# Causal attention and a hard-swish block on one core: five token groups become four of 448

## The chip, the cores and the metric

The kernel runs on one core of one Trainium2 chip. The metric is the device time of one execution in microseconds (us), as the median of several executions. TensorE (PE) multiplies; VectorE (DVE), ScalarE (ACT) and GpSimd (POOL) do elementwise work; SyncE (SP) issues every DMA of this kernel.

## The reference

Causal attention over 4 batches, 12 heads, 448 tokens and 64 dimensions a head, all in fp32, and behind it two matrix products with a hard-swish between them over the 1792 tokens:

```
scores = (q @ k.T) / 8, with -1e9 above the diagonal
attn   = exp(scores - rowmax) / (rowsum + 1e-9)
x      = (attn @ v), the heads side by side: 1792 x 768
h      = x @ w_in                      # 768 x 2048
g      = h * clip(h + 3, 0, 6) / 6
out    = g @ w_out                     # 2048 x 768
```

## The kernel before

**Tokens.** A sequence is cut into four blocks of C = 112 tokens, S = 448, R = 336. The two products behind the attention (the FFN from here on) are done for groups of tokens, with the weights stationary and the tokens of the group as the columns that stream. Group 0 holds the first block of all four batches (448 columns). Groups 1 to 4 hold blocks 1 to 3 of one batch each (336 columns).

**Attention.** Heads are taken two at a time (NPAIR = 6 pairs). `first_pair(p)` (L297) does group 0's attention for one pair, where only the diagonal blocks count. `pair(n)` (L410) does blocks 3, 2 and 1 of one batch and one pair: the scores (`products`, L445: matmuls L450 and L451, or L453), a masked row maximum on DVE (L476), the exponential on ACT (L483), the reciprocal of the row sums on DVE (L492, L493), the scaling on POOL (L505), the transposes of the 112x112 blocks on PE (L516), their eviction to SBUF (`move`, L238 or L241), and attention times V (`times_v`, L535). For batch 0 the scores are plain fp32 matmuls of 64 rows a head (L453). For batches 1 to 3 the operands are split into a rounded and a rest part (tiles op and kl, lines L245 and L250) and two matmuls a head and block do the product. The 64-row and 64-column matmuls (L453, L535, L399) use PE as several smaller arrays; the planner charges `SWITCH` for going to or from that mode (`tiled`). `x_split` (L277) evicts the result and splits it into xh and xl.

**FFN.** `group(g)` (L602) makes the group's two products. Every product of 128x128 weights with the tokens is three matmuls, high with high (L598), high with rest (L599), rest with high (L600). The up projection takes 16 chunks of weights with 18 matmuls each, the down projection 6 outputs with 48 each: 576 matmuls a group. `weights` (L547) loads a chunk of weights and splits it into wh (ACT) and wl (POOL or DVE). In group 0 DVE also decodes the words in which the weights arrive (L571, L573, L576), and the decoded ones are stored (kept_w) and loaded again by the later groups.

**Order.** Nothing runs in program order. Every piece of work is an `Op` with a key, the engines that may do it, a planned duration and its buffers. `Flow.run` plays the kernel through as a list schedule: a free engine takes the ready operation of the lowest key whose buffers (`BUFS`, L54; PSUM banks, `BANKS`, L58) are free, and the order that comes out is emitted for each engine. The keys count FFN steps: a group has 96 steps of six matmuls, group g begins at key 96 g. `pair(n)` begins at `T_EARLY + 13 * n` for batch 0 and at `T_REST + 16 * n` after it, its attention times V stands 15.9 steps later, its loads 24 steps before (`T_LOAD`). `first_pair(p)` begins at `T_FIRST + 8 * p`. So the attention of group g fills in between the FFN steps of group g-1.

```
T_FIRST, T_EARLY, T_REST, T_LOAD, T_W, T_WLOAD = -66, 4, -16, -24, 9, 9
t = T_FIRST + 8 * p
t = T_REST + 16 * n if b else T_EARLY + 13 * n
```

Of the kernel before, what the change touches and what calls it, by code (L numbers as in the profile page):

```python
# [33 lines left out]
F32R = mybir.dt.float32r  # L34
# [16 lines left out]
T_FIRST, T_EARLY, T_REST, T_LOAD, T_W, T_WLOAD = -66, 4, -16, -24, 9, 9  # L51
# [3 lines left out]
    gh=1, gl=1, prow=3, r=4, qk=4, op=3, kl=3, vr=3, wh=3, wl=3, pr3=4, pr2=3, pr1=3,  # L55
    pt0=4, pt1=4, pt2=4, wd=4, xh=8, xl=8,
# [134 lines left out]
def tile_causal_attention_hardswish_moe(ctx: ExitStack, tc: tile.TileContext, q, k, v, w_in, w_out, out):  # L191
# [85 lines left out]
    def x_split(key, g, p, av, n):  # L277
        xh, xl = buf("xh", [128, S], F32R), buf("xl", [128, S], F32R)
        x_t[g, p] = xh, xl
        move(key, n, lambda: ap(xh)[:, :n], lambda: ap(av)[:, :n], [(av, 0)], [(xh, 0)], {"A": 1, "D": (1, .5)})  # L280
        y = av
        if g < 2:
            y = buf("r", [128, S])
            move(key, n, lambda: ap(y)[:, :n], lambda: ap(av)[:, :n], [(av, 0)], [(y, 0)], {"A": 1})
        minus(
            key + .01, n, lambda: ap(xl)[:, :n], lambda: ap(y)[:, :n], lambda: f(ap(xh)[:, :n]),
            [(y, 0), (xh, 0)], [(xl, 0)], {"P": 2.4, "D": (1, 1.0)} if g < 2 else {"D": 1},
        )
# [8 lines left out]
    def first_pair(p):  # L297
        t = T_FIRST + 8 * p
# [11 lines left out]
        pr, ph = [buf("pr3", [C, S]) for _ in range(2)], [buf("pt0", [C, S]) for _ in range(2)]  # L310
# [97 lines left out]
    TILES = (3, 2, 1)  # L408

    def pair(n):  # L410
        b, p = divmod(n, NPAIR)
        t = T_REST + 16 * n if b else T_EARLY + 13 * n
        vr = buf("vr", [C, NC_, 2, D])
        qk = [buf("qk", [128, R + S]) for _ in range(2 if b else 1)]
        for e, x in enumerate(qk):
            for src, c0, c1 in ((q, C, 0), (k, 0, R)):
                n = S - c0
                for u in range(2):
                    dma(
                        t + T_LOAD, 256 * n, lambda x=x, u=u, c1=c1, n=n: ap(x)[64 * u:64 * u + 64, c1:c1 + n],  # L420
                        lambda e=e if b else u, src=src, c0=c0: src[b, p, e, :, c0:], w=[(x, u, c1)],
                    )
        dma(t + T_LOAD, 230e3, lambda: ap(vr), lambda: v[b, p], w=[(vr, 0)])
        raw = [(x, u, c1) for x in qk for u in range(2) for c1 in (0, R)]
        op, kl = [[buf(a, [128, w], F32R) for _ in qk] for a, w in (("op", R + S), ("kl", S))]
        if b:
            for e in range(2):
                x, y, z = qk[e], op[e], kl[e]
                move(
                    t - 5, R + S, lambda x=x, y=y: ap(y), lambda x=x: ap(x), raw[4 * e:4 * e + 4] + [("step", t - 12)], [(y, 0), (y, 1)],  # L430
                    {"P": 1.3, "A": (1, .5)},
                )
                minus(
                    t - 4.9, S, lambda z=z: ap(z), lambda x=x: ap(x)[:, R:], lambda y=y: f(ap(y)[:, R:]),
                    [(x, 0, R), (x, 1, R), (y, 1)], [(z, 0)], {"D": 1.25, "P": (2.2, 1.5)},
                )
                minus(
                    t - 4.8, R, lambda y=y: ap(y)[64:, :R], lambda x=x: ap(x)[64:, :R], lambda y=y: f(ap(y)[64:, :R]),
                    [(x, 1, 0)], [(y, 0)], {"D": 1.3, "P": (2.6, 1.5)},
                )  # L440
        st = buf("prow", [C, 2, 8])
        ps = {(e, i): bank("s") for i in TILES for e in range(2)}
        pr = {(e, i): buf(f"pr{i}", [C, C * (i + 1)]) for i in TILES for e in range(2)}

        def products(i, heads=(0, 1)):  # L445
            w, c = C * (i + 1), slice(C * (i - 1), C * i)
            for e in heads:
                dst, m = ap(ps[e, i])[:C, :w], slice(64 * e, 64 * e + 64)
                if b:
                    nc.tensor.matmul(dst, ap(op[e])[:, c], ap(op[e])[:, R:R + w], start=True, stop=False)  # L450
                    nc.tensor.matmul(dst, ap(op[e])[:, c], ap(kl[e])[:, :w], start=False, stop=True)  # L451
                else:
                    nc.tensor.matmul(dst, ap(qk[0])[m, c], ap(qk[0])[m, R:R + w], start=True, stop=True)  # L453

        for j, tiles in enumerate(((3, 2), (1,))):
            if b:
                for i in tiles:
                    for e in range(2):
                        pe(
                            t + 2 * j + .01 * e, [(.907e-3 * C * (i + 1), lambda i=i, e=e: products(i, (e,)), [(ps[e, i], 0), ("turn",)])],  # L460
                            [(op[e], 0), (op[e], 1), (kl[e], 0)],
                        )
            else:
                pe(
                    t + 2 * j,
                    [((1.68 * C * (i + 1) + 170) / 1000, lambda i=i: products(i), [(ps[0, i], 0), (ps[1, i], 0), ("turn",)])
                     for i in tiles],
                    raw, True,
                )
            for i in tiles:  # L470
                w = C * (i + 1)
                for e in range(2):
                    dst = lambda e=e, i=i, w=w: ap(ps[e, i])[:C, :w]
                    one(
                        t + 2 * j + .1, {"D": 1}, elem(w) + .2,
                        lambda _, e=e, i=i, w=w, dst=dst: nc.vector.tensor_tensor_reduce(  # L476
# [5 lines left out]
                        t + 2 * j + .2, {"A": 1}, (w + 300) / 1200 + .25,  # L482
                        lambda _, e=e, i=i, dst=dst: nc.scalar.activation(  # L483
# [6 lines left out]
        def inverse(_):  # L490
            r = ap(st)[:, :, 5:8]
            nc.vector.tensor_scalar_add(r, r, 1e-9)  # L492
            nc.vector.reciprocal(r, r)  # L493

        sums = [(st, e, 4 + i) for e in range(2) for i in TILES]
        one(t + 4, {"D": 1}, .45, inverse, [], sums)
        pt = {}
        for e in range(2):
            for i in reversed(TILES):
                def scaled(g, e=e, i=i):  # L500
                    x, r = ap(pr[e, i]), ap(st)[:, e, 4 + i:5 + i]
                    if g == "A":
                        nc.scalar.mul(x, x, r)
                    else:
                        nc.gpsimd.tensor_scalar(x, x, r, 1.0, ALU.mult, ALU.mult)  # L505
                one(
                    t + 4.5 + .1 * e, {"P": 1}, min(.95, .2 + C * (i + 1) / 500), scaled,
                    [(st, e, 4 + i)], [(pr[e, i], 0)],
                )
            for a, js in enumerate(((0,), (1,), (2, 3))):  # L510
                blocks = [(i, j) for j in js for i in range(max(j, 1), NC_)]
                tp, ph = bank("s"), buf(f"pt{js[0]}", [C, S] if js[0] == 0 else [C, R])

                def turn(e=e, blocks=blocks, tp=tp):
                    for o, (i, j) in enumerate(blocks):
                        nc.tensor.transpose(ap(tp)[:C, C * o:C * o + C], ap(pr[e, i])[:, C * j:C * j + C], ident)  # L516

                key = t + 6 + 3 * e + a
                pe(key, [(.3, turn, [(tp, 0)])], [(pr[e, i], 0) for i in {i for i, _ in blocks}])
                move(  # L520
                    key + .1, R, lambda ph=ph: ap(ph)[:, :R], lambda tp=tp: ap(tp)[:C, :R],
                    [(tp, 0)], [(ph, 0)], {"A": 1, "D": (1, .4)} if b else {"A": 1},
                )
                o = 0
                for j in js:
                    w = R if j == 0 else S - C * j
                    pt[e, j] = ph, o, w
                    o += w
        av = bank("s")

        def times_v():
            for j in range(NC_):
                for e in range(2):
                    ph, o, w = pt[e, j]
                    nc.tensor.matmul(  # L535
                        ap(av)[64 * e:64 * e + 64, R - w:R], ap(vr)[:, j, e, :], ap(ph)[:, o:o + w],
                        start=(j == 0), stop=(j == NC_ - 1),
                    )
# [63 lines left out]
    def group(g):  # L602
        n, t0 = (R if g else S), 96 * g
# [34 lines left out]
        for m in range(NK):  # L638
# [18 lines left out]
            if g:  # L657
# [52 lines left out]
```

## Time and profile before

| | |
|---|---|
| median of 3 runs | 660.11 us (659.89 to 660.64) |
| the profiled execution | 661.54 us |
| its span, first to last instruction | 659.8 us |
| mean granted clock of TensorE | 0.992 |
| PE / DVE / ACT / POOL busy, of the span | 98% / 71% / 56% / 46% |

The 1.7 us between the span and the execution's own time lie around the program. Busy PE is counted from matmuls that overlap, so the rows below are read by the starts of matmuls rather than by their durations. A line L598 is line 598 of the kernel; where a helper records an operation (`move`, `minus`), its tiles tell which one it is.

### The profile page before, as it was taken

How to read it: one execution, taken by the hardware profiler on the slowest of the kernel's cores; microseconds unless marked ns; L12 is line 12 of the kernel's file. 1: busy time of each engine (PE TensorE's matmuls, PEld its weight loads, DVE VectorE, ACT ScalarE, POOL GpSimd, SP SyncE). 2: the span in 40 equal slices, each digit the busy share in tenths (PEclk: the TensorE clock that was granted, in tenths of full speed). 3: DMA queues.
4: the chain of work that ended last, by engine and by line, in shares of the span. 5: the costliest groups of instructions: out<-in, count | busy, mean ns of one | idle time of the engine just before them, and what ended most of it. 6: DMA issues, size and time to landing. Idle time of an engine off the chain costs nothing.

```text
span 659.8 us, 12245 instructions
## 1 busy us (share of the span) xinstructions
PE 643.9 (98%) x4236; PEld 587.3 (89%) x4236; DVE 465.8 (71%) x939; ACT 367.3 (56%) x870; POOL 301.2 (46%) x333
## 2 busy tenths in 40 slices
PE   7689999999999999999999999999999999999998
PEld 5569887878889999999999999999999999999997
DVE  4889898977687798854588795567798743566432
ACT  3665656654546666555576664656666554444342
POOL 1667667546572686423375563433676410011100
PEclk9979999999999999999999999999999999999999
DMA  9989876888788543556744547555553334643452
GB/s 232 259 267 298 265 242 192 260 282 295 206 265 246 158 144 107 159 171 182 217 152 135 154 127 206 157 168 186 161 168 87 112 113 132 209 139 110 139 164 65
DMA packets 66878, 120.89 MB, mean 183 GB/s; under 512 B 16896, under 2 KB 33408, under 8 KB 66816
## 3 DMA queue, kind: packets, MB, share of 16 engines
q1 hardware_dynamic: 66816, 120.11, 60.7%
q8 instruction: 33, 0.54, 0.3%
q14 instruction: 29, 0.24, 0.1%
HBM read 101.99 MB, written 18.09 MB: 182 GB/s over the span
## 4 chain that ended last, share of the span: by engine, by line
PE 92%; DVE 3%; DMA 1%; SPq 1%; ACT 1%; POOL 1%; issue 1%; DVEq 0%; ACTq 0%; POOLq 0%
PE mo L598 24%; PE mo L600 23%; PE mo L599 23%; PE s L535 6%; PE s L516 6%; PE s L450 3%; PE s L451 2%; PE s L453 2%; DMA gh<-in_k_dram 1%; SPq L229 1%; PE s L399 1%; DVE s L571 1%; DVE s L573 1%; DVE op L576 0%; PE s L329 0%
## 5 line engine op out<-in xcount | busy, mean ns | idle before, releaser
L250 DVE TENSOR_TENSOR wl<-wd,wh 128x512 fp32r<-128x512 f32 (+1 forms) x159 | 142.8, 898 | 99.8 <-ACT wh L238 99.5
L238 ACT CAST wh<-wd 128x512 fp32r<-128x512 f32 (+1 forms) x160 | 112.9, 706 | 120.0 <-PE mo L599 85.9
L598 PE MATMUL mo<-xh,wh 128*128 128x336 f32 (+1 forms) x480 | 160.8, 335 | 0.1
L598 PE MATMUL mo<-gh,wh 128*128 128x336 f32 (+1 forms) x480 | 159.2, 332 | 0.0
L600 PE MATMUL mo<-xh,wl 128*128 128x336 f32 (+1 forms) x480 | 157.2, 327 | 0.0
L600 PE MATMUL mo<-gh,wl 128*128 128x336 f32 (+1 forms) x480 | 156.9, 327 | 0.3 <-POOL wl L250 0.3
L599 PE MATMUL mo<-gl,wh 128*128 128x336 f32 (+1 forms) x480 | 156.4, 326 | 0.0
L599 PE MATMUL mo<-xl,wh 128*128 128x336 f32 (+1 forms) x480 | 156.2, 325 | 0.0
L505 POOL TENSOR_SCALAR pr<-pr,prow 112x224 f32<-112x224 f32 x144 | 109.0, 773 | 39.5 <-DVE prow L493 39.3
L476 DVE CUSTOM_DVE_ANT_0 s<-s,mask 112x448 f32<-112x448 f32 (+1 forms) x144 | 70.6, 527 | 39.7 <-PE s L451 33.1
L245 POOL TENSOR_SCALAR gh<-r 128x336 fp32r<-128x336 f32 x51 | 33.3, 654 | 138.2 <-DVE r L627 128.6
L598 PEld LDWEIGHTS mo<-xh,wh 128*128 128x128 f32 x480 | 91.0, 190 | 5.8 <-issue 1.7
L598 PEld LDWEIGHTS mo<-gh,wh 128*128 128x128 f32 x480 | 90.3, 188 | 2.8 <-issue 0.8
L599 PEld LDWEIGHTS mo<-xl,wh 128*128 128x128 f32 x480 | 91.4, 190 | 1.1
L600 PEld LDWEIGHTS mo<-gh,wl 128*128 128x128 f32 x480 | 90.2, 188 | 2.2 <-POOL wl L250 0.6
L600 PEld LDWEIGHTS mo<-xh,wl 128*128 128x128 f32 x480 | 90.6, 189 | 1.3
L599 PEld LDWEIGHTS mo<-gl,wh 128*128 128x128 f32 x480 | 90.3, 188 | 1.3
L483 ACT ACTIVATE pr<-s,prow 112x448 f32<-112x448 f32 (+1 forms) x144 | 76.9, 542 | 25.7 <-DVE prow L476 25.7
L250 POOL TENSOR_TENSOR wl<-op,wh 128x512 fp32r<-128x512 f32 (+1 forms) x35 | 53.3, 1522 | 44.1 <-ACT wh L238 34.3
L238 ACT COPY pt<-s 112x336 f32<-112x336 f32 x139 | 53.3, 446 | 26.0 <-PE s L516 25.9
L621 ACT ACTIVATE r<-mo,three 128x336 f32<-128x336 f32 (+1 forms) x80 | 44.7, 558 | 26.4 <-PE mo L600 20.9
L245 POOL TENSOR_SCALAR op<-qk 128x784 fp32r<-128x784 f32 x31 | 30.4, 985 | 57.3 <-PE s L451 54.0
(70 smaller groups left out, 853.6 us busy)
## 6 DMA issues: line engine op xcount, KB each, us to landing
wd<-kept_w SPq DMA_DIRECT2D x64, 384.0 KB, 3.3
wd<-kept_w SPq DMA_DIRECT2D x96, 256.0 KB, 2.7
wd<-in_w_in_dram SPq DMA_DIRECT2D x16, 768.0 KB, 5.7
wd<-in_w_out_dram SPq DMA_DIRECT2D x24, 512.0 KB, 5.2
qk<-in_k_dram SPq DMA_DIRECT2D x84, 112.0 KB, 2.7
qk<-in_q_dram SPq DMA_DIRECT2D x84, 84.0 KB, 2.6
kept_w<-op SPq DMA_DIRECT2D x16, 384.0 KB, 5.7
kept_w<-op SPq DMA_DIRECT2D x24, 256.0 KB, 5.4
```

What stands on the lines that cost most here:

```text
L238: nc.scalar.copy(o(), i()) if scale is None else nc.scalar.mul(o(), i(), scale)
L245: nc.gpsimd.tensor_scalar(o(), i(), 1.0, 1.0, ALU.mult, ALU.mult)
L250: (nc.gpsimd if e == "P" else nc.vector).tensor_tensor(o(), a(), b(), ALU.subtract)
L476: lambda _, e=e, i=i, w=w, dst=dst: nc.vector.tensor_tensor_reduce(dst(), dst(), mask[:, S - w:], -0.125, 3.0e38, ALU.add, ALU.min, ap(st) ...
L483: lambda _, e=e, i=i, dst=dst: nc.scalar.activation(ap(pr[e, i]), dst(), ACTF.Exp, bias=ap(st)[:, e, i:i + 1], scale=-1.0, accum_out=ap(st ...
L505: nc.gpsimd.tensor_scalar(x, x, r, 1.0, ALU.mult, ALU.mult)
L516: nc.tensor.transpose(ap(tp)[:C, C * o:C * o + C], ap(pr[e, i])[:, C * j:C * j + C], ident)
L535: nc.tensor.matmul(ap(av)[64 * e:64 * e + 64, R - w:R], ap(vr)[:, j, e, :], ap(ph)[:, o:o + w], start=(j == 0), stop=(j == NC_ - 1),)
L598: nc.tensor.matmul(ps, ap(wh)[:, a], xh, start=start, stop=False)
L599: nc.tensor.matmul(ps, ap(wh)[:, a], xl, start=False, stop=False)
L600: nc.tensor.matmul(ps, ap(wl)[:, a], xh, start=False, stop=stop)
L621: lambda _, r=r, acc=acc: nc.scalar.activation(ap(r)[:, :n], ap(acc)[:, :n], ACTF.Relu, bias=three, scale=1.0),
```

## The change

The tokens of batches 1 to 3 are dealt to the groups in another way, so that there are four groups of 448 columns. Group 0 stays. Group 1 takes blocks 3, 2, 1 of batch 0 and block 1 of batch 1, group 2 blocks 3, 2 of batch 1 and 2, 1 of batch 2, group 3 block 3 of batch 2 and 3, 2, 1 of batch 3. `pair(n)`, 24 of them, becomes `unit(g, p)`, 18 of them, with a piece for each of its two batches. A piece has its own loads (the columns of q that it needs, k and v up to its last block), its own operands, statistics and V; both write one PSUM bank, side by side, and one `x_split` of 448 columns takes it. Block 1 of batch 1 is now done with plain fp32 matmuls. A unit has eight score blocks a pair of heads in place of six, made in two steps of two blocks, and eight evictions of transposes; they stand 0.9 steps apart. Units begin at `T_EARLY + 14 * n` with `T_EARLY` 2, and `T_REST + 16 * n` with `T_REST` -5. `first_pair` begins at 7 steps a pair instead of 8. The three tags of transposed tiles become one of ten buffers; `prow` has four. An output tile is stored with one DMA for each piece. The diff, cut:

```diff
-T_FIRST, T_EARLY, T_REST, T_LOAD, T_W, T_WLOAD = -66, 4, -16, -24, 9, 9
+T_FIRST, T_EARLY, T_EACH, T_REST, T_LOAD, T_W, T_WLOAD = -66, 2, 14, -5, -24, 9, 9
-    gh=1, gl=1, prow=3, r=4, qk=4, op=3, kl=3, vr=3, wh=3, wl=3, pr3=4, pr2=3, pr1=3,
-    pt0=4, pt1=4, pt2=4, wd=4, xh=8, xl=8,
+    gh=1, gl=1, prow=4, r=4, qk=4, op=3, kl=3, vr=3, wh=3, wl=3, pr3=4, pr2=3, pr1=3,
+    pt=10, wd=4, xh=8, xl=8,
...
-        t = T_FIRST + 8 * p
+        t = T_FIRST + 7 * p
...
+    UNITS = {
+        1: ((0, (3, 2, 1), ((0,), (1,), (2, 3))), (1, (1,), ((0, 1),))),
+        2: ((1, (3, 2), ((0, 1), (2, 3))), (2, (2, 1), ((0, 1), (2,)))),
+        3: ((2, (3,), ((0, 1, 2, 3),)), (3, (3, 2, 1), ((0,), (1,), (2, 3)))),
+    }
+
+    def unit(g, p):
+        n = NPAIR * (g - 1) + p
+        raw32 = g == 1
+        t = T_EARLY + T_EACH * n if raw32 else T_REST + 16 * n
+        av, off = bank("s"), 0
+        stages, turns, pieces, deps = [], [], [], []
+        for u, (b, tiles, groups) in enumerate(UNITS[g]):
+            lo, hi = tiles[-1], tiles[0] + 1
+            nq, nk = C * len(tiles), C * hi
+            vr = buf("vr", [C, NC_, 2, D])
+            qk = [buf("qk", [128, R + S]) for _ in range(1 if raw32 else 2)]
+            for e, x in enumerate(qk):
+                for src, c0, c1, n in ((q, C * lo, 0, nq), (k, 0, nq, nk)):
+                    for h in range(2):
+                        dma(
...
+            dma(t + T_LOAD, 512 * nk, lambda vr=vr, hi=hi: ap(vr)[:, :hi], lambda b=b, hi=hi: v[b, p, :, :hi], w=[(vr, 0)])
...
+                    if raw32:
+                        nc.tensor.matmul(dst, ap(qk[0])[m, c], ap(qk[0])[m, nq:nq + w], start=True, stop=True)
+                    else:
+                        nc.tensor.matmul(dst, ap(op[e])[:, c], ap(op[e])[:, nq:nq + w], start=True, stop=False)
+                        nc.tensor.matmul(dst, ap(op[e])[:, c], ap(kl[e])[:, :w], start=False, stop=True)
...
+                        nc.tensor.matmul(
+                            ap(av)[64 * e:64 * e + 64, off + nq - w:off + nq], ap(vr)[:, j, e, :], ap(ph)[:, o:o + w],
+                            start=(j == 0), stop=(j == hi - 1),
+                        )
+
+            cost = sum(pt[0, j][2] for j in range(hi)) * 1.77e-3
+            pieces.append((cost, times_v, [(av, u)]))
...
+        for a in range(0, len(stages), 2):
+            two, key = stages[a:a + 2], t + a
...
+        for c, (e, u, blocks, pr, ph, w, st) in enumerate(turns):
+            tp, key = bank("s"), t + 6 + .9 * c
...
+        pe(t + 15.9, pieces, deps, True)
+        x_split(t + 16, g, p, av, S)
...
-        n, t0 = (R if g else S), 96 * g
+        n, t0 = S, 96 * g
...
+            o = 0
+            for b, tiles, _ in UNITS.get(g, ()):
+                w, c = C * len(tiles), C * tiles[-1]
+                dma(
+                    t + 1, 512 * w, lambda rows=rows, b=b, c=c, w=w: rows[:, b, c:c + w],
+                    lambda ob=ob, o=o, w=w: ap(ob)[:, o:o + w], [(ob, 0)],
+                )
+                o += w
+            if not g:
                 dma(t + 1, 230e3, lambda rows=rows: rows[:, :, :C], lambda ob=ob: by_batch(ap(ob)), [(ob, 0)])
...
-    for g in range(B + 1):
+    for g in range(B):
         if g:
             for p in range(NPAIR):
-                pair(NPAIR * (g - 1) + p)
+                unit(g, p)
```

## Rows read from the trace of the kernel before

**Rows 1.** The page: busy time of each engine, and the chain by engine.

```profile
PE 643.9 (98%) x4236; PEld 587.3 (89%) x4236; DVE 465.8 (71%) x939; ACT 367.3 (56%) x870; POOL 301.2 (46%) x333
...
PE 92%; DVE 3%; DMA 1%; SPq 1%; ACT 1%; POOL 1%; issue 1%; DVEq 0%; ACTq 0%; POOLq 0%
```

**Rows 2.** Busy time by stretch: us, PE, PEld, DVE, ACT, POOL, granted clock, DMA share, GB/s.

```profile
45.00:205.00 160.00, 159.20 (x888) 133.29 (x886) 136.55 (x281) 88.66 (x209) 101.22 (x103) 0.99 0.82 261
205.00:328.00 123.00, 123.00 (x857) 115.87 (x854) 87.55 (x180) 74.55 (x179) 59.67 (x67) 1.00 0.56 165
```

**Rows 3.** PE's timeline, group 0's up projection: start, duration, instruction; 34 intervals.

```profile
55.13 0.37 PE L598 MATMUL mo<-xh,wh 128*128 128x448 f32 x1
...
61.93 0.36 PE L599 MATMUL mo<-xl,wh 128*128 128x448 f32 x1
```

**Rows 4.** PE's timeline, group 0's down projection; 30 intervals.

```profile
126.84 0.36 PE L598 MATMUL mo<-gh,wh 128*128 128x448 f32 x1
...
132.96 0.36 PE L598 MATMUL mo<-gh,wh 128*128 128x448 f32 x1
```

**Rows 5.** PE's timeline, the last group, 336 columns; 42 intervals.

```profile
630.25 0.31 PE L598 MATMUL mo<-gh,wh 128*128 128x336 f32 x1
...
636.69 0.31 PE L598 MATMUL mo<-gh,wh 128*128 128x336 f32 x1
```

**Rows 6.** PE's timeline, split-operand scores of block 1: first and last of four.

```profile
270.96 0.26 PE L450 MATMUL s<-op 128*112 128x224 f32 x1
...
271.27 0.26 PE L451 MATMUL s<-kl,op 128*112 128x224 f32 x1
```

**Rows 7.** PE's timeline, plain fp32 scores of block 1 and what follows.

```profile
142.57 0.64 PE L453 MATMUL s<-qk 64*112 64x224 f32 x4
143.14 1.92 PE L535 MATMUL s<-pt,vr 112*64 112x336 f32 x16
```

**Rows 8.** PE's timeline around one attention times V (L535), 1008 columns in all.

```profile
266.26 0.37 PE L451 MATMUL s<-kl,op 128*112 128x448 f32 x1
266.56 1.92 PE L535 MATMUL s<-pt,vr 112*64 112x336 f32 x16
268.41 0.41 PE L450 MATMUL s<-op 128*112 128x336 f32 x1
268.66 0.32 PE L451 MATMUL s<-kl,op 128*112 128x336 f32 x1
```

**Rows 9.** PE's timeline at the start: first scores of pair(0), last first_pair, first FFN.

```profile
33.62 2.96 PE L453 MATMUL s<-qk 64*112 64x448 f32 x8
...
44.28 0.99 PE L399 MATMUL s<-pt,gl 112*64 112x112 f32 x16 [1.80 <-ACT pr L483]
45.20 0.48 PE L598 MATMUL mo<-xh,wh 128*128 128x448 f32 x1
```

**Rows 10.** PE's timeline, one run of transposes and the FFN matmuls behind it.

```profile
261.11 1.03 PE L516 MATMUL s<-ident,pr 112*112 112x112 f32 x9
261.91 0.40 PE L598 MATMUL mo<-xh,wh 128*128 128x336 f32 x1
262.15 0.32 PE L599 MATMUL mo<-xl,wh 128*128 128x336 f32 x1
```

**Rows 11.** All engines' timeline, the end: last eviction and last store.

```profile
656.67 0.45 ACT L238 ACTIVATE r<-mo 128x336 f32<-128x336 f32 x1 [5.05 <-PE mo L600]
657.14 0.34 SPq L229 DMA_DIRECT2D out_dram<-r  x1
```

**Rows 12.** DVE's groups by shape, 45 to 195 us: busy us, mean ns | idle before.

```profile
L476 DVE DVE_READ_ACCUMULATOR2_ANT prow<- 112x1 f32 x39 | 5.5, 142 | 0.0
L476 DVE CUSTOM_DVE_ANT_0 s<-s,mask 112x224 f32<-112x224 f32 x14 | 5.3, 416 | 2.8 <-PE s L453 2.8
L492 DVE TENSOR_SCALAR prow<-prow 112x6 f32<-112x6 f32 x7 | 3.3, 466 | 0.0
L493 DVE RECIPROCAL prow<-prow 112x6 f32<-112x6 f32 x7 | 1.3, 191 | 0.2
```

More of the change, by code (lines that the diff above doesn't have):

```diff
@@ L309, in first_pair @@
         st, ps = buf("prow", [C, 2, 8]), [bank("s") for _ in range(2)]
-        pr, ph = [buf("pr3", [C, S]) for _ in range(2)], [buf("pt0", [C, S]) for _ in range(2)]
+        pr, ph = [buf("pr3", [C, S]) for _ in range(2)], [buf("pt", [C, S]) for _ in range(2)]
         sc = [lambda e=e: by_batch(ap(ps[e])[:C, :S]) for e in range(2)]
@@ L405, in first_pair @@
         x_split(t + 14.5, 0, p, av, S)
[L408 to L421, printed above, removed]
-                    )
[L423 to L426, printed above, removed]
-            for e in range(2):
[L428 to L431, printed above, removed]
-                )
[L433 to L457, printed above, removed]
@@ new lines, in tile_causal_attention_hardswish_moe, with products, times_v @@
+    UNITS = {
[3 rows of a table added]
+    }
[14 more added lines that the diff above has]
+                        dma(
+                            t + T_LOAD, 256 * n, lambda x=x, h=h, c1=c1, n=n: ap(x)[64 * h:64 * h + 64, c1:c1 + n],
+                            lambda e=h if raw32 else e, src=src, c0=c0, n=n, b=b: src[b, p, e, :, c0:c0 + n],
+                            w=[(x, h, bool(c1))],
+                        )
+            dma(t + T_LOAD, 512 * nk, lambda vr=vr, hi=hi: ap(vr)[:, :hi], lambda b=b, hi=hi: v[b, p, :, :hi], w=[(vr, 0)])
+            raw = [(x, h, c) for x in qk for h in range(2) for c in (False, True)]
+            op = kl = None
+            if not raw32:
+                op, kl = [[buf(a, [128, w], F32R) for _ in qk] for a, w in (("op", R + S), ("kl", S))]
+                for e in range(2):
+                    x, y, z = qk[e], op[e], kl[e]
+                    key = t - 5 + 2 * u
+                    move(
+                        key, nq + nk, lambda x=x, y=y, m=nq + nk: ap(y)[:, :m], lambda x=x, m=nq + nk: ap(x)[:, :m],
+                        raw[4 * e:4 * e + 4] + [("step", t - 12 + 2 * u)], [(y, 0), (y, 1)], {"P": 1.3, "A": (1, .5)},
+                    )
+                    minus(
+                        key + .1, nk, lambda z=z, m=nk: ap(z)[:, :m], lambda x=x, o=nq, m=nk: ap(x)[:, o:o + m],
+                        lambda y=y, o=nq, m=nk: f(ap(y)[:, o:o + m]),
+                        [(x, 0, True), (x, 1, True), (y, 1)], [(z, 0)], {"D": 1.25, "P": (2.2, 1.5)},
+                    )
+                    minus(
+                        key + .2, nq, lambda y=y, m=nq: ap(y)[64:, :m], lambda x=x, m=nq: ap(x)[64:, :m],
+                        lambda y=y, m=nq: f(ap(y)[64:, :m]), [(x, 1, False)], [(y, 0)], {"D": 1.3, "P": (2.6, 1.5)},
+                    )
+            st = buf("prow", [C, 2, 8])
+            ps = {(e, i): bank("s") for i in tiles for e in range(2)}
+            pr = {(e, i): buf(f"pr{i}", [C, C * (i + 1)]) for i in tiles for e in range(2)}
+            def products(i, heads=(0, 1), lo=lo, nq=nq, qk=qk, op=op, kl=kl, ps=ps):
+                w, c = C * (i + 1), slice(C * (i - lo), C * (i - lo + 1))
+                for e in heads:
+                    dst, m = ap(ps[e, i])[:C, :w], slice(64 * e, 64 * e + 64)
+                    if raw32:
[3 more added lines that the diff above has]
+                        nc.tensor.matmul(dst, ap(op[e])[:, c], ap(kl[e])[:, :w], start=False, stop=True)
+            stages += [(u, i, products, ps, pr, st, raw, op, kl) for i in tiles]
+            pt = {}
+            for e in range(2):
+                for js in groups:
+                    blocks = [(i, j) for j in js for i in range(max(j, lo), hi)]
+                    ph, o = buf("pt", [C, S]), 0
+                    for j in js:
+                        w = C * (hi - max(j, lo))
+                        pt[e, j] = ph, o, w
+                        o += w
+                    turns.append((e, u, blocks, pr, ph, o, st))
+            def times_v(hi=hi, nq=nq, off=off, pt=pt, vr=vr):
+                for j in range(hi):
+                    for e in range(2):
+                        ph, o, w = pt[e, j]
+                        nc.tensor.matmul(
+                            ap(av)[64 * e:64 * e + 64, off + nq - w:off + nq], ap(vr)[:, j, e, :], ap(ph)[:, o:o + w],
+                            start=(j == 0), stop=(j == hi - 1),
+                        )
+            cost = sum(pt[0, j][2] for j in range(hi)) * 1.77e-3
+            pieces.append((cost, times_v, [(av, u)]))
+            deps += [(vr, 0)] + [(x[0], 0) for x in pt.values()]
+            off += nq
+        for a in range(0, len(stages), 2):
+            two, key = stages[a:a + 2], t + a
+            if raw32:
+                pe(
+                    key,
+                    [((1.68 * C * (i + 1) + 170) / 1000, lambda i=i, go=go: go(i), [(ps[0, i], 0), (ps[1, i], 0), ("turn",)])
+                     for _, i, go, ps, *_ in two],
+                    [x for z in two for x in z[6]], True,
+                )
+            else:
+                for _, i, go, ps, _, _, _, op, kl in two:
@@ L458, in pair @@
                     for e in range(2):
                         pe(
[L460 removed]
+                            key + .01 * e, [(.907e-3 * C * (i + 1), lambda i=i, e=e, go=go: go(i, (e,)), [(ps[e, i], 0), ("turn",)])],
                             [(op[e], 0), (op[e], 1), (kl[e], 0)],
                         )
[L463 to L469, printed above, removed]
@@ L470, in pair @@
-            for i in tiles:
+            for u, i, _, ps, pr, st, *_ in two:
                 w = C * (i + 1)
                 for e in range(2):
-                    dst = lambda e=e, i=i, w=w: ap(ps[e, i])[:C, :w]
+                    dst = lambda e=e, i=i, w=w, ps=ps: ap(ps[e, i])[:C, :w]
                     one(
-                        t + 2 * j + .1, {"D": 1}, elem(w) + .2,
-                        lambda _, e=e, i=i, w=w, dst=dst: nc.vector.tensor_tensor_reduce(
+                        key + .1, {"D": 1}, elem(w) + .2,
+                        lambda _, e=e, i=i, w=w, dst=dst, st=st: nc.vector.tensor_tensor_reduce(
@@ L488, in pair @@
                     )
[L490 to L537, printed above, removed]
-                    )
-        pe(t + 15.9, [(1.9, times_v, [(av, 0)])], [(vr, 0)] + [(x[0], 0) for x in pt.values()], True)
-        x_split(t + 16, b + 1, p, av, R)
+        for u, (b, tiles, _) in enumerate(UNITS[g]):
+            st, pr = [(z[5], z[4]) for z in stages if z[0] == u][0]
+            def inverse(_, st=st, tiles=tiles):
+                r = ap(st)[:, :, 4 + tiles[-1]:5 + tiles[0]]
+                nc.vector.tensor_scalar_add(r, r, 1e-9)
+                nc.vector.reciprocal(r, r)
+            one(t + 4, {"D": 1}, .45, inverse, [], [(st, e, 4 + i) for e in range(2) for i in tiles])
+            for e in range(2):
+                for i in reversed(tiles):
+                    def scaled(_, e=e, i=i, st=st, pr=pr):
+                        x = ap(pr[e, i])
+                        nc.gpsimd.tensor_scalar(x, x, ap(st)[:, e, 4 + i:5 + i], 1.0, ALU.mult, ALU.mult)
+                    one(
+                        t + 4.5 + .1 * e + .2 * u, {"P": 1}, min(.95, .2 + C * (i + 1) / 500), scaled,
+                        [(st, e, 4 + i)], [(pr[e, i], 0)],
+                    )
@@ new lines, in unit, with turn @@
+        for c, (e, u, blocks, pr, ph, w, st) in enumerate(turns):
+            tp, key = bank("s"), t + 6 + .9 * c
+            def turn(e=e, blocks=blocks, tp=tp, pr=pr):
+                for o, (i, j) in enumerate(blocks):
+                    nc.tensor.transpose(ap(tp)[:C, C * o:C * o + C], ap(pr[e, i])[:, C * j:C * j + C], ident)
+            pe(key, [(.1 * len(blocks), turn, [(tp, 0)])], [(pr[e, i], 0) for i in {i for i, _ in blocks}])
+            move(
+                key + .1, w, lambda ph=ph, w=w: ap(ph)[:, :w], lambda tp=tp, w=w: ap(tp)[:C, :w],
+                [(tp, 0)], [(ph, 0)], {"A": 1} if raw32 else {"A": 1, "D": (1, .4)},
+            )
```

15 lines of the change are left out of this document (7 added, 8 removed).

## The prediction

> **What bounds the kernel now.** I read the page's busy line and its chain first. PE is busy 98% of the span and holds 92% of the chain [rows 1]. The table by stretch shows where: from 205 us on PE is never idle, and in group 0's stretch, 45 to 205 us, it lacks 0.8 us of 160 [rows 2]. No other engine is near that, except DVE in group 0: 136.55 of 160 us, 85%, because there it also decodes the weights. In the next group DVE has 87.55 of 123, POOL 59.67, and the DMA engines are at 0.56 [rows 2]. Before 45 us PE waits for the first blocks' attention; the first FFN matmul starts at 45.20 [rows 9]. So the time is 45 us of start, some 611 us of PE issuing matmuls, and a tail of 3 us. The change is priced by what it does to PE's issue, then by whether the others keep pace. Since matmuls overlap in the profile, a matmul's cost is the distance between starts.
>
> **FFN matmuls.** Before, 4 x 576 = 2304 matmuls have 336 columns; after, 3 x 576 = 1728 have 448. Columns are the same: 774,144. A 336-column matmul takes 6.44 us / 42 = 153.3 ns [rows 5]. One of 448 takes 6.80 / 34 = 200.0 ns in the up projection [rows 3], but 6.12 / 30 = 204.0 ns in the down projection [rows 4], both at a granted clock of 0.99 or more. Half of a group's matmuls are up, half down. Before: 2304 x 0.1533 = 353.2 us. After: 864 x 0.2000 + 864 x 0.2040 = 349.1. That is **-4.1 us**. All at 200.0 would be 345.6, or -7.6; all at 204.0, 352.5, or -0.7. I take the split, since it is what each projection shows at this width, and keep both ends. From 336 to 448 columns the up cadence grows by 46.7 ns, 0.417 ns a column (2.4 GHz), which leaves 153.3 - 140.0 = 13.3 ns a matmul that does not depend on its width. That part, paid 576 times less, is the gain; the slower down projection gives half of it back.
>
> The Trainium skill ("TensorE: Matmul & The Clock Gate", Back-to-back issue gap) says a warm matmul's start-to-start distance is its columns at 2.4 GHz plus about 2.5 ns. By it 576 fewer matmuls would save 1.4 us instead of 4.1. The rows disagree with it here: 13.3 ns.
>
> **Scores.** Block 1 of batch 1 leaves the split form: four matmuls of 0.31 / 3 = 0.103 us each [rows 6], 0.41 a pair, six pairs, -2.5 us. It enters the plain form: 0.57 for the two heads [rows 7], of which some 0.2 is the change of PE's mode (below); as it stands in the same PE operation as block 1 of batch 0, that is already paid: 0.37 x 6 = +2.2. Together **-0.3**, at worst +0.9 if it comes alone. The other scores keep their number and width.
>
> **Attention times V.** The columns stay, but 24 runs become 18. Entering the mode costs 0.30 - 0.20 = 0.10, leaving it 0.25 - 0.15 = 0.10 [rows 8]: 6 x 0.2 = -1.2. Against it, splitting batches makes narrow steps: a pair column now has ten 112-wide ones where it had four, 36 more in all. Four such steps took 45.20 - 44.28 = 0.92, 0.23 each [rows 9], where 112 columns of a long run cost 1.85 x 112 / 1008 = 0.21 [rows 8]: between 0 and 0.02 x 36 = +0.9. I take **-0.3**, the upper one, and keep -1.2.
>
> **Transposes.** 432 blocks and 144 evictions before and after. What can change is how often PE goes back to the FFN: the first matmul behind a run takes 0.24 in place of 0.153, so 0.09 a run [rows 10]. Before there are mostly two runs a pair, 48. After, each piece and head becomes ready by itself: at most four a unit, 72, +2.1; if pieces merge, 36, -1.1. I take **+0.5**.
>
> **The tail.** The last eviction has 448 columns, 0.45 x 448 / 336 = 0.60 at most, and the last store is two DMAs, so the second is issued 0.34 later [rows 11]: **+0.4**, between 0 and +0.5.
>
> **Start.** Seven steps instead of eight move pair p+1's maxima ahead of pair p's evictions on DVE and ACT; both rank ahead of the weights before and after, so little changes hands. Unit 0 brings four more score matmuls in front of the last first blocks; its first eight took 2.96 us there [rows 9], half of that is +1.5. On the other side the last attention times V waits 1.80 us for ACT [rows 9]; no better order saves more than about that. I take **0**, between -1.8 and +1.5.
>
> **Other queues.** SP issues 10 loads a unit in group 1 and 18 in groups 2 and 3 where a pair had 5 and 9: 276 in place of 192. It saves 40 loads of weights and adds 12 stores. At 0.34 us an issue [rows 11], 56 more are 19 us spread over 600 on a queue that nobody waits for while loads are keyed 24 steps ahead. POOL and DVE prepare 48 sets of split operands where they had 36, on three `op` buffers that a unit needs four of; so its last operand is copied only after its first products. FFN steps of 1.2 us cover that, as POOL has half its time free and DVE 29% [rows 2]; I cost it at nothing. If that cover failed, PE would wait in line for a unit's products with the FFN behind them.
>
> **DVE in group 0.** A unit of group 1 has two more score blocks and a second reciprocal: 2 x (0.416 + 0.142) + 0.466 + 0.191 = 1.77 us [rows 12], six units 10.6. Its PE work grows by 4 x 0.09 + 0.37 + 0.41 = 1.14, six times 6.8. So DVE goes from 136.6 of 160 to 147.2 of 166.8, 88%. That leaves 12% idle, and I take **+0.5** for a wait here and there.
>
> **Sum:** -4.1 - 0.3 - 0.3 + 0.5 + 0.4 + 0 + 0.5 = -3.3 us, against a profiled execution of 661.54 us (span 659.8). The median of the runs shown is 1.4 lower; the difference is put to the median: 660.11 - 3.3 = **656.8 us**. A measurement of this kernel tells about 0.2%, 1.3 us, from no change: faster is under 658.8, slower over 661.4.
>
> **Rivals.**
> - *The down projection's 204.0 ns belongs to group 0 alone*, as its decoding does; with 336 columns both projections of later groups run alike. Then all later matmuls take 200.0 and the gain is 3.5 larger: 653.3. Against it: the 204.0 stands evenly through the stretch, whatever DVE does. Chance 0.18.
> - *Columns cost the same at both widths in later groups.* The 200.0 stands early in group 0 and the 204.0 late, so 204.0 could hold for both projections from there on: -0.7 in place of -4.1, 660.2, no change. Against it: 336 columns cost 153.3 late in the same execution, with no sign of a slower PE [rows 5]. Chance 0.16. By the rule of the Trainium skill named above ("TensorE: Matmul & The Clock Gate"), with 1.4 us saved in the FFN, the time would be 659.5, on this rival's side.
> - *DVE takes PE's place in group 0.* Its idle time there may be waits that can't be filled. If it keeps its idle share of 14.7%, 147.2 us of work need 172.5, 5.7 more than PE's 166.8: 660.11 - 3.8 + 5.7 = 662.0, slower. It decides against the change once DVE cannot be filled beyond about 86%. For it: DVE is the only engine near its limit, and in-order queues make every late row maximum a PE wait. Against it: PE lost only 0.8 us in that stretch. Chance 0.17.
>
> What is left, 0.05, is a start later by several us, which also ends slower. The forecast has 0.44. Of that I count 0.06 as within 0.2%, since its small terms reach 658.8. Faster: 0.38 + 0.18 + some 0.02 of the second rival, 0.58. Within: 0.06 + 0.14 + 0.02 = 0.22. Slower: 0.20. The range takes in the first rival with part of a shorter start, 652.0, and the third with a later start, 663.0; the likeliest case alone has 654.5 to 659.0.
>
> **What would show it.** The changed kernel's timeline should give 200.0 ns in the up projection and 204.0 in the down projection of groups 1 to 3. The first FFN matmul should start within 2 us of 45.2. In group 0's stretch, longer by some 7 us, PE should stay at 99% and DVE near 88%. Nowhere behind that should PE be idle. Wrong would be a first FFN start several us away, idle PE with DVE as its releaser in group 0, PE waiting for L450 operands in groups 1 and 2, or a cadence of 448 columns that fits neither value.

## The result and the profile after

The changed kernel ran at 653.1 us, median of 5 (651.98 to 656.43), the kernel before beside it at 660.64 (659.89 to 661.92). The ratio is 0.9895, 95% interval 0.9865 to 0.9925: faster, by some 7 us. The profiled execution is the shortest of the five, while that of the kernel before took 661.54, 0.9 over its median here, so the two profiles differ by more than the medians.

The page of the changed kernel, busy time and the chain by engine, as in [rows 1]:

```profile
PE 632.6 (97%) x3780; PEld 559.5 (86%) x3780; DVE 441.0 (68%) x919; ACT 337.2 (52%) x795; POOL 291.5 (45%) x326
...
PE 91%; DVE 4%; DMA 2%; ACT 1%; issue 1%; POOL 1%; SPq 0%; DVEq 0%; POOLq 0%; ACTq 0%
```

Its busy time by stretch (columns as in [rows 2]): the start, and groups 0 to 3:

```profile
0.00:49.00 49.00, 36.60 (x278) 26.11 (x279) 37.59 (x89) 27.63 (x90) 21.26 (x26) 0.93 0.90 241
49.00:208.00 159.00, 157.58 (x931) 133.99 (x930) 133.00 (x287) 91.07 (x221) 99.55 (x105) 1.00 0.81 260
208.00:370.00 162.00, 162.00 (x996) 146.82 (x995) 116.42 (x257) 92.51 (x221) 83.34 (x93) 1.00 0.55 156
370.00:531.00 161.00, 161.00 (x1005) 144.74 (x1004) 105.47 (x218) 88.04 (x205) 76.93 (x87) 1.00 0.46 135
531.00:646.00 115.00, 115.00 (x577) 107.80 (x576) 48.50 (x70) 37.39 (x59) 10.38 (x17) 1.00 0.36 105
```

PE is still the bound: never idle behind 208 us, and 1.4 us short in group 0's stretch, where DVE is busy 84%. The same table of the kernel before, for its start and its last group, whose 576 matmuls have 336 columns:

```profile
0.00:45.20 45.20, 33.27 (x265) 24.61 (x265) 31.93 (x74) 24.98 (x82) 20.42 (x24) 0.92 0.93 241
567.50:656.30 88.80, 88.80 (x577) 88.10 (x576) 43.60 (x71) 35.86 (x60) 8.39 (x16) 1.00 0.46 135
```

The FFN's cadence, PE's timeline of the changed kernel: twelve intervals of group 0's down projection, and 39 of group 3's up projection, to be held against [rows 4] and [rows 3]:

```profile
154.00 0.36 PE L622 MATMUL mo<-gh,wl 128*128 128x448 f32 x1
...
156.40 0.36 PE L622 MATMUL mo<-gh,wl 128*128 128x448 f32 x1
...
559.65 0.36 PE L622 MATMUL mo<-xh,wl 128*128 128x448 f32 x1
...
567.45 0.36 PE L622 MATMUL mo<-xh,wl 128*128 128x448 f32 x1
```

2.40 / 12 and 7.80 / 39 are both 200.0 ns. The matmuls of group 0's down projection are the same in both kernels; they had 204.0 before and have 200.0 now. That was not forecast. The later groups' down projections, forecast at 204.0, run like it; the last one stands by itself, without any attention:

```profile
588.64:646.05 57.41, 57.41 (x289) 53.81 (x287) 15.73 (x23) 16.44 (x28) 1.87 (x2) 1.00 0.36 103
```

57.41 / 288 is 199.3 ns.

Adding up the distances between matmul starts in both profiles (us; the spans are 659.8 and 650.2):

| part | forecast | measured |
|---|---|---|
| first FFN matmul, 45.20 to 48.68 | 0 | +3.5 |
| FFN, 481.9 to 472.5 | -4.1 | -9.3 |
| scores behind the first FFN matmul, 45.7 to 42.1 | -0.3 | -3.7 |
| attention times V, 44.4 to 43.7 | -0.3 | -0.8 |
| transposes, 39.1 to 39.1 | +0.5 | 0.0 |
| tail from the last matmul's start, 3.5 to 4.1 | +0.4 | +0.6 |

The start and the scores belong together: unit 1's first scores now stand in front of the first FFN matmul, and 3.2 us of scores have moved ahead of it. PE's timeline of the changed kernel there, to be held against [rows 9]:

```profile
43.98 1.47 PE L399 MATMUL s<-pt,gl 112*64 112x112 f32 x16 [0.17 <-ACT pr L525]
46.51 2.24 PE L464 MATMUL s<-qk 64*112 64x448 f32 x8 [1.07 <-ACT r L238]
48.68 0.48 PE L620 MATMUL mo<-xh,wh 128*128 128x448 f32 x1
```

The last first block is as early as before.

Of the FFN's -9.3, 7.0 stand in the later groups and 2.3 in group 0. Some 1.5 of these 2.3 come from the clock, and not from the matmuls' width or place: in the kernel before's profile the granted clock stood at 0.50, the 1.2 GHz level, from 45.9 to 49.3 us; PE had last waited 1.80 us just before its first FFN matmul [rows 9]. Nine FFN matmuls took 3.34 us there, where nine at 200.0 ns take 1.80:

```profile
45.91 0.56 PE L598 MATMUL mo<-xh,wh 128*128 128x448 f32 x1
...
49.25 0.41 PE L598 MATMUL mo<-xh,wh 128*128 128x448 f32 x1
```

In the changed kernel's profile the clock is at 1.00 from the first FFN matmul on. Whether the change does that stays open; experiment 6 shows the slow clock in a run that differs from the changed kernel in the last group alone. So the gain lies in the FFN, and the experiments ask why it is twice the forecast.

### The profile page after: what moved, and what is told of

Its sections match the earlier page's. It is cut to its first block, busy times and chain, and to the rows that moved or that the text cites. A ratio compares the mean times of both kernels' runs of the same rounds, so it can differ in the third digit from the quotient of the medians.

```text
span 650.2 us, 11293 instructions
## 1 busy us (share of the span) xinstructions
PE 632.6 (97%) x3780; PEld 559.5 (86%) x3780; DVE 441.0 (68%) x919; ACT 337.2 (52%) x795; POOL 291.5 (45%) x326
## 4 chain that ended last, share of the span: by engine, by line
PE 91%; DVE 4%; DMA 2%; ACT 1%; issue 1%; POOL 1%; SPq 0%; DVEq 0%; POOLq 0%; ACTq 0%
PE mo L620 24%; PE mo L621 23%; PE mo L622 23%; PE s L486 7%; PE s L555 6%; PE s L466 2%; PE s L467 2%; PE s L464 2%; DMA gh<-in_k_dram 1%; PE mo L386 1%; DMA kept_w<-op 1%; DVE op L598 1%; PE s L399 1%; DVE s L595 1%; PE s L329 1%
## 5 line engine op out<-in xcount | busy, mean ns | idle before, releaser
L620 PE MATMUL mo<-gh,wh 128*128 128x448 f32 x384 | 143.1, 373 | 0.0
L620 PE MATMUL mo<-xh,wh 128*128 128x448 f32 x384 | 143.0, 372 | 0.0
L622 PE MATMUL mo<-xh,wl 128*128 128x448 f32 x384 | 139.0, 362 | 0.2 <-DVE wl L250 0.2
L621 PE MATMUL mo<-xl,wh 128*128 128x448 f32 x384 | 139.3, 363 | 0.0
L621 PE MATMUL mo<-gl,wh 128*128 128x448 f32 x384 | 139.3, 363 | 0.0
L622 PE MATMUL mo<-gh,wl 128*128 128x448 f32 x384 | 139.1, 362 | 0.0
L545 POOL TENSOR_SCALAR pr<-pr,prow 112x224 f32<-112x224 f32 (+2 forms) x144 | 102.6, 730 | 39.3 <-DVE prow L538 35.6
L518 DVE CUSTOM_DVE_ANT_0 s<-s,mask 112x448 f32<-112x448 f32 (+2 forms) x144 | 70.3, 530 | 21.4 <-PE s L467 17.2
L525 ACT ACTIVATE pr<-s,prow 112x448 f32<-112x448 f32 (+2 forms) x144 | 76.8, 540 | 13.8 <-DVE prow L518 11.6
L555 PE MATMUL s<-ident,pr 112*112 112x112 f32 x432 | 53.8, 260 | 1.2 <-DVE op L598 0.6
```

What stands on the lines that cost most here:

```text
L518: lambda _, e=e, i=i, w=w, dst=dst, st=st: nc.vector.tensor_tensor_reduce(dst(), dst(), mask[:, S - w:], -0.125, 3.0e38, ALU.add, ALU.min, ...
L525: lambda _, e=e, i=i, dst=dst, st=st, pr=pr: nc.scalar.activation(ap(pr[e, i]), dst(), ACTF.Exp, bias=ap(st)[:, e, i:i + 1], scale=-1.0, a ...
L545: nc.gpsimd.tensor_scalar(x, x, ap(st)[:, e, 4 + i:5 + i], 1.0, ALU.mult, ALU.mult)
L620: nc.tensor.matmul(ps, ap(wh)[:, a], xh, start=start, stop=False)
L621: nc.tensor.matmul(ps, ap(wh)[:, a], xl, start=False, stop=False)
L622: nc.tensor.matmul(ps, ap(wl)[:, a], xh, start=False, stop=stop)
```

## The experiments

**1. Both kernels again.** No edit.

> The kernel before, unchanged, profiled a second time. In the first profile its group 0 took 200.0 ns a matmul in the up projection and 204.0 in the down projection. Theory 1 (the 204.0 belongs to one execution): both projections near 200.0 to 200.5 here, and the span about 1 us shorter, near 658.8. Theory 2 (it belongs to the program, by where its tiles lie or what else runs then): 204.0 again, span near 659.8.

> The changed kernel, unchanged, profiled a second time. Its five timed runs fell into two lots, 652.0 to 653.1 and 656.3 to 656.4. Theory 1 (the 204.0 ns cadence comes and goes between executions): a run near 656 has a group or two at 204 where the first profile had 200.0 to 200.9, 288 matmuls x 4 ns = 1.2 us for each projection; a run near 652 has none. Theory 2 (the start differs, by when the first loads land): cadences as in the first profile, and the first FFN matmul starts later by the difference, at about 52 us instead of 48.7.

The kernel before took 660.41 us, span 658.7. PE's timeline in its group 0's down projection, 27 intervals:

```profile
125.07 0.36 PE L598 MATMUL mo<-gh,wh 128*128 128x448 f32 x1
...
130.57 0.37 PE L598 MATMUL mo<-gh,wh 128*128 128x448 f32 x1
```

5.50 / 27 = 203.7 ns: theory 2, the 204 belongs to the program. The changed kernel took 651.67 us with all cadences as in its first profile, so it leaves open why two of its five timed runs took some 4 us more.

**2. The small edits alone, in the kernel before (b_space7), and the spacing undone in the changed one (a_space8).**

```diff
-    gh=1, gl=1, prow=3, r=4, qk=4, op=3, kl=3, vr=3, wh=3, wl=3, pr3=4, pr2=3, pr1=3,
+    gh=1, gl=1, prow=4, r=4, qk=4, op=3, kl=3, vr=3, wh=3, wl=3, pr3=4, pr2=3, pr1=3,
...
-        t = T_FIRST + 8 * p
+        t = T_FIRST + 7 * p
```

```diff
-        t = T_FIRST + 7 * p
+        t = T_FIRST + 8 * p
```

> The kernel before with the two small edits alone: the first blocks 7 steps apart and four prow buffers instead of three. My theory: within 1.5 us of the kernel before, as the gain is in the FFN's wider matmuls. Rival (the small edits carry part of the gain): 2 to 4 us faster, with an earlier first FFN matmul. If the 204.0 ns cadence hangs on where tiles lie in memory, the 64 bytes a partition that prow adds may also move group 0's down projection from 204.0 to 200.

> The changed kernel with the first six blocks 8 steps apart again instead of 7. My theory (the spacing changes little): within 1.5 us of the changed kernel, first FFN matmul within 2 us of 48.7, everything behind it the same. Rival (the spacing is a part of the gain): first FFN matmul later, the kernel slower by 2 to 4 us.

The small edits made the kernel before slower: 667.28, ratio 1.0103 (1.0078 to 1.0129). Neither theory had that. The spacing undone gave 655.05, ratio to the kernel before 0.9923 (0.9899 to 0.9946), some 2 us behind the changed kernel though the intervals overlap: between theory and rival, and a gain of the spacing is not shown. Neither had the start right: the first FFN matmul came at 42.64, six us earlier, and nothing of it was left. The first nine FFN matmuls ran at a granted clock of 0.50 (42.8 to 46.3 us), group 0 took 164.6 us in place of 159.7, with more of the scores in it, and group 1 3.5 us more, 1.6 of it PE idle.

**3. The two small edits apart, in the kernel before: the buffer (b_prow4) and the spacing (b_only7).**

```diff
-    gh=1, gl=1, prow=3, r=4, qk=4, op=3, kl=3, vr=3, wh=3, wl=3, pr3=4, pr2=3, pr1=3,
+    gh=1, gl=1, prow=4, r=4, qk=4, op=3, kl=3, vr=3, wh=3, wl=3, pr3=4, pr2=3, pr1=3,
```

```diff
-        t = T_FIRST + 8 * p
+        t = T_FIRST + 7 * p
```

> The kernel before with four prow buffers alone. The two small edits together made it 6.8 us slower (667.28 against 660.45) and took group 0's down projection from 203.7 to 200.4 ns a matmul. Theory 1 (the fourth buffer moves the tiles behind it in memory, and the cadence hangs on that): 200.4 in group 0's down projection here; time within 1.5 us of the kernel before. Theory 2 (the cadence hangs on the order that the planner makes of the spacing): 203.7 here, 200.4 with the spacing alone.

> The kernel before with the first blocks 7 steps apart alone. Theory 1 (the spacing makes a worse order in the kernel before, PE waiting at about 188 to 203 us for the weights of the group change): 665 to 668 us, those waits present, and the down projection of group 0 still at 203.7. Theory 2 (the buffer makes the waits): within 1.5 us of 660.45.

The spacing alone is the loss: 667.57, ratio 1.0112 (1.0092 to 1.0132), first FFN matmul at 43.20, and group 0's down projection at 203.9. Who PE waits for at the change from group 0 to group 1, 180 to 210 us (us in total, times, longest):

```profile
PE s L450 <- ACT wh L238: 1.1, 1, 1.1
PE mo L600 <- DVE wl L250: 1.0, 1, 1.0
PE mo L598 <- ACT wh L238: 0.6, 1, 0.6
PE s L450 <- DVE op L250: 0.4, 1, 0.4
PE mo L600 <- POOL wl L250: 0.4, 1, 0.4
```

These are 3.5 us of the 6.6; the kernel before has one such wait of 0.3 in that window, and where the rest went was not traced. A key moved by one step at the start came out as a worse order 150 us later.

The fourth buffer alone changed no engine's order, instruction for instruction, and gave 659.24, ratio 0.9983 (0.9969 to 0.9997). PE's timeline, group 0's down projection, 33 intervals:

```profile
126.58 0.36 PE L598 MATMUL mo<-gh,wh 128*128 128x448 f32 x1
...
133.18 0.36 PE L598 MATMUL mo<-gh,wh 128*128 128x448 f32 x1
```

6.60 / 33 = 200.0 ns. Theory 1 in both: the cadence goes with the buffer, the waits with the spacing.

**4. The place or the buffer?** An unused tile of 64 bytes a partition, as much as one prow buffer, behind three prow buffers in both kernels (b_pad, a_pad; the diff is that on the changed one); and the changed kernel with three and no more (a_prow3, the first line of `BUFS` with `prow=3` alone).

```diff
-    gh=1, gl=1, prow=4, r=4, qk=4, op=3, kl=3, vr=3, wh=3, wl=3, pr3=4, pr2=3, pr1=3,
+    gh=1, gl=1, prow=3, pad=1, r=4, qk=4, op=3, kl=3, vr=3, wh=3, wl=3, pr3=4, pr2=3, pr1=3,
...
-    three = const.tile([128, 1], F32, tag="three", name="three")
+    three = const.tile([128, 1], F32, tag="three", name="three"); pad = pools["pad"].tile([C, 2, 8], F32, tag="pad", name="pad")
...
-        nc.vector.memset(three, 3.0)
+        nc.vector.memset(three, 3.0); nc.vector.memset(pad, 0.0)
```

> The kernel before with its three prow buffers and an unused tile of 64 bytes a partition behind them; the order stays the same. Theory 1 (placement): group 0's down projection at 200.3 ns as with the fourth prow buffer, the time about 1 us under the kernel before. Theory 2 (the fourth buffer helped by being free earlier, not by its place): 203.7.

> The changed kernel with three prow buffers instead of four; the order of every engine stays the same. In the kernel before, the fourth buffer alone took group 0's down projection from 203.7 to 200.3 ns with the order unchanged. Theory 1 (where the tiles behind prow lie sets the cadence of 448-column matmuls): the down projections of all four groups at about 204, 4 x 288 x 3.4 ns = 3.9 us slower. Theory 2 (the placement mattered only for the kernel before): cadences at 200.0 to 200.9 as with four buffers, time within 1 us.

> The changed kernel with three prow buffers and an unused tile of 64 bytes a partition behind them, which puts every later tile back where the fourth buffer had it. Three buffers alone ran at 659.62 with all down projections at 203.3 to 204.0 ns; four at 653.1 with 199.3 to 200.7. Theory 1 (the place of the tiles is all that the fourth buffer gives): 200 ns in every down projection and 652 to 656 us. Theory 2 (the buffer itself is needed): about 200 ns but some 2 to 3 us slower than 653.1. Theory 3 (the 653.1 was a lucky lot of runs): 200 ns and near 656 to 658, the cadence's 3.8 us under 659.62.

The kernel before with the pad: 659.51, ratio 0.9981 (0.9970 to 0.9993), as with the fourth buffer, and 200.0 ns: 1.80 for nine intervals.

```profile
126.32 0.36 PE L598 MATMUL mo<-gh,wh 128*128 128x448 f32 x1
...
128.12 0.36 PE L598 MATMUL mo<-gh,wh 128*128 128x448 f32 x1
```

The changed kernel with three buffers: 659.62 (656.91 to 662.52, 12 runs), ratio 0.9975 (0.9957 to 0.9992). With three and the pad: 654.62, ratio 0.9894 (0.9871 to 0.9918), the changed kernel's own 0.9895. The tables by stretch show the last group's down projection, 288 matmuls without any attention: three buffers, then three and the pad; the changed kernel itself has 57.41 (above).

```profile
593.38:651.93 58.55, 58.55 (x289) 53.91 (x287) 15.69 (x23) 16.41 (x28) 1.86 (x2) 1.00 0.35 101
```

```profile
591.38:648.78 57.40, 57.40 (x288) 53.81 (x287) 15.69 (x23) 16.42 (x28) 1.88 (x2) 1.00 0.36 103
```

58.55 / 288 is 203.3 ns, 57.40 / 288 is 199.3. DVE, ACT and POOL did the same work. So the place of the tiles behind prow sets the cadence of the down projections with 448 columns, and no free buffer is needed. The four down projections took 239.4 us with three buffers and 235.7 with four: 3.8 us. The median moved by 6.5, or by 5.0 against the run with the pad. The two ratios' intervals leave 2.6 to 8 us for the pad, so 3.8 is enough, and nothing shows that the place gives more than the cadence. With three buffers the FFN of groups 1 to 3 took 4.1 us less than the 336-column groups of the kernel before, as the forecast has it.

**5. How much room does DVE have in group 0?** Extra DVE work behind the reciprocals of group 1's units; in the second run (the last two lines of the diff) 1.05 us of it for each is told to the planner. The results of the extra work go nowhere.

```diff
+    spare = const.tile([C, S], F32, tag="spare", name="spare")
...
+                if raw32:
+                    for _ in range(2):
+                        nc.vector.tensor_tensor(spare, mask, mask, ALU.subtract)
...
-            one(t + 4, {"D": 1}, .45, inverse, [], [(st, e, 4 + i) for e in range(2) for i in tiles])
+            one(t + 4, {"D": 1}, 1.5 if raw32 else .45, inverse, [], [(st, e, 4 + i) for e in range(2) for i in tiles])
```

> The changed kernel with two subtractions of 112x448 more on DVE behind every reciprocal of group 1's units, 24 in all and unknown to the planner; their results go nowhere. At some 0.6 us each that is 14 us, more than the 10.6 that the change itself adds to DVE in group 0's stretch. My theory (PE bounds that stretch, DVE has 26 us to spare of 159): slower by under 3 us. Rival (DVE's idle time there can't be filled): slower by 8 to 14 us, with DVE as PE's releaser.

> The run with two more DVE subtractions behind each reciprocal of group 1's units, now with 1.05 us more for each reciprocal told to the planner. The 24 took 25.0 us of DVE in the first run and made the kernel 15 us slower. Theory 1 (DVE has room, but each engine works in a fixed order, so only work that the planner counts is covered): under 6 us slower than the changed kernel. Theory 2 (DVE with 25 us more is the bound of group 0's stretch, 158 of 159 us): 10 to 15 us slower again.

668.55 and 668.58, ratios to the kernel before 1.0126 (1.0104 to 1.0149) and 1.0114 (1.0092 to 1.0135): 15 us behind the changed kernel, planned or not. The first theory fell in both. The subtractions were dearer than I had thought, by DVE's groups in the first run:

```profile
L542 DVE TENSOR_TENSOR spare<-mask 112x448 f32<-112x448 f32 x24 | 25.0, 1041 | 0.4
```

The stretch of group 0 in that run, and whom PE waited for most in it:

```profile
50.30:222.90 172.60, 163.58 (x934) 137.12 (x934) 157.63 (x310) 90.50 (x220) 105.25 (x105) 0.98 0.76 239
```

```profile
PE s L559 <- DVE op L602: 4.9, 2, 3.0
PE s L559 <- ACT pr L526: 2.0, 2, 1.5
PE mo L626 <- DVE wl L250: 1.1, 1, 1.1
```

DVE is busy 157.63 of 172.60 us, 91%, and the stretch is 12.9 us longer than the changed kernel's 159.7. About 10 of the 25 us were covered. PE's idle time in the stretch is 9.0 us, where the changed kernel has 1.4. Some 3 us more went to the clock: twice the granted clock fell to 0.50, the 1.2 GHz level (106.2 to 109.7 and 133.5 to 137.0 us), each time behind such waits, and a matmul then takes 0.37 us in place of 0.20. So the price of 15 us holds both, the waits and the slower clock that followed them.

**6. The fixed cost of a matmul.** The last group's matmuls in two halves.

```diff
+        for h in halves:
+            nc.tensor.matmul(ps[:, h], ap(wh)[:, a], xh[:, h], start=start and h is halves[0], stop=False)
...
+        halves = [slice(0, S // 2), slice(S // 2, S)] if g == B - 1 else [slice(0, S)]
...
```

> The changed kernel with every FFN matmul of the last group cut into two of 224 columns, 1152 in place of 576 on the same columns. My theory (13.3 ns a matmul whatever its width): 106.7 ns each, the group's 115.0 us become 122.9, the kernel 7.7 us slower. By the fixed 2.5 ns of the Trainium skill (TensorE: Matmul & The Clock Gate, Back-to-back issue gap) it would be 1.4 us slower. A third possibility is that the weight load, 188 ns a piece in the records, sets a floor above 107 ns: then slower by more than 8 us.

668.28 us, ratio 1.0115 (1.0092 to 1.0137), 15 us behind the changed kernel. The group's stretch:

```profile
534.50:663.02 128.52, 128.52 (x1153) 128.52 (x1151) 48.50 (x70) 37.37 (x59) 10.35 (x17) 1.00 0.32 94
```

128.5 in place of 115.0: 13.5 us, neither 7.7 nor 1.4. The 1.4 came from a formula that the Trainium skill ("TensorE: Matmul & The Clock Gate", Back-to-back issue gap) gives for an isolated matmul; of a stream of weight loads and matmuls, as here, the section says that both set the spacing.

A matmul of 224 columns takes 128.52 / 1152 = 111.6 ns, 18.2 over its columns at 2.4 GHz. So the run can't test the 13.3: something else sets the pace at this width. The third possibility, the weight load, fits: PEld fills the stretch without a gap, as it does not at 448 columns (107.80 of 115.00 above). That alone does not show it, for at 336 columns PEld is nearly as full (88.10 of 88.80 above) while the cadence is 13.3 over the columns. What speaks for it is that the split-operand scores [rows 6], also 224 columns but with 112 stationary ones, take 103. The Trainium skill ("TensorE: Matmul & The Clock Gate", LDWEIGHTS) gives a load columns / 1.2 ns, by which one would estimate 106.7 for 128 and 93.3 for 112; both rows lie 5 to 10 ns above that and keep its order.

That leaves 1.7 us of the 15 elsewhere. In this execution the first FFN matmuls ran at a granted clock of 0.50, the changed kernel's at 1.00. First this run, then the changed kernel, for a stretch as long:

```profile
47.80:52.10 4.30, 4.30 (x12) 3.80 (x12) 4.00 (x8) 0.00 (x0) 1.36 (x1) 0.50 0.86 196
```

```profile
48.70:53.00 4.30, 4.30 (x23) 4.03 (x23) 4.00 (x8) 0.65 (x2) 1.85 (x1) 1.00 0.62 142
```

Twelve matmuls in place of 23: such a start costs some 2 us. It may be one part of the 4 us by which the runs of one kernel differ; no run tests that.

## Why the prediction was right, and where its steps were not

The time fell in the range and went the way forecast, 653.1 for 656.8. But it came out at the first rival's 653.3, for a reason that no rival named, and that this reason worked in the forecast's direction is luck. With three `prow` buffers the same change gave 659.62, which the forecast's own bounds call no change.

- *FFN matmuls, -4.1: mis-sized.* The 200.0 of the up projection held in the later groups, and with it the 13.3 ns over the columns at both widths. "I take the split, since it is what each projection shows at this width" failed: the 204.0 was the mark of a place in memory, and the change moved the tiles by giving prow a fourth buffer. The measured term is -9.3: 7.0 in the later groups, of which 4.1 is the width and 2.9 the place, and 2.3 in group 0, of which some 1.5 is the clock at the start of the kernel before's profile. With three buffers the forecast's split came true in all groups, 200.0 up and 203.3 to 204.0 down. By the cadences, 3.8 of the 7 us are the tiles' place; the whole change with three buffers is worth 0.25% (0.08 to 0.43).
- *The fourth `prow` buffer* stands in the change, but the prediction has no term for it, so it was put at nothing without a reason. No wait hung on it, and the order stayed the same; its 64 bytes were the largest thing that the sum lacked.
- *First rival.* Right in its number, wrong in "belongs to group 0 alone": with the old layout every group has it. *Second rival*, 204.0 in both projections: no run has it.
- *Start, 0.* The sign, within 2 us of 45.2, failed: 48.68. The size fits once the scores that moved ahead are counted. The reason was wrong: seven steps do change hands, in the planner's order further on. Alone they cost the kernel before 6.6 us; in the changed one they are within the noise.
- *Scores, attention times V, tail.* -0.5 in all for the scores, -0.8 and +0.6, against -0.3, -0.3 and +0.4. *Transposes* kept their 39.1 us; PE goes back to the FFN from them 64 times where it did 47, 1.5 us by [rows 10], inside the FFN's term.
- *DVE in group 0, +0.5.* PE lacks 1.4 us in that stretch where it lacked 0.8, but the load that the term was worked out for did not come. DVE was busy 133.0 us, 84%, not 147.2 and 88%, and the stretch did not grow by 7 us: 576 FFN matmuls took 159.7 us there where they took 160.1. Part of the work had moved ahead of the first FFN matmul, 37.59 us of DVE where it was 31.93. That DVE had 12% to give was too much: 25 us more cost 15, so the third rival's mechanism exists; it begins somewhere between 84% and 91%. *Operands in groups 1 and 2* are covered as said: no PE wait behind 208 us.

No version here beats the changed kernel; the one with the pad equals it.

## What to carry to other kernels

Where PE issues without a gap, the cadence between matmul starts, taken for each shape and each operand, prices a change of width better than busy time; fewer and wider matmuls pay by what does not scale with the width. A cadence that differs between two uses of one shape is to be explained before it is carried over: here it hung on 64 bytes of padding, which is cheap to try. In a kernel whose order a list scheduler makes, a small key is no small edit, and has to be run by itself.

## What the runs showed of the hardware

- A 448-column matmul of 128x128 weights takes 200.0 or 204.0 ns in the down projection, by the place of the tiles behind prow in SBUF, at a granted clock of 1.00. The 336-column ones stay at 153 to 154 in both layouts tried. Which tile it is was not tried. `BUFS` offers a reading: the streaming tiles gh and gl are listed ahead of prow, the weights wh and wl and the up projection's xh and xl behind it. If they lie in that order, 64 bytes more move the weights against gh and gl, but move the up projection's weights and streaming tiles together. That is not shown.
- At 224 columns and 128 stationary ones a matmul takes 111.6 ns with the weight loads back to back.
- The granted clock stood at 0.50 at the start of the FFN in some profiles, and behind PE's waits in the run with more DVE work; a 448-column matmul then took 0.37 us in place of 0.20.
- A subtraction of 112x448 on DVE from SBUF took 1041 ns in the mean of 24 (583 to 2991), where a 448-column reduction from PSUM takes 0.6 us. Why was not tried.
